# Another order table for a linear-attention and MoE kernel on one core

## The chip, the cores and the metric

The kernel runs on one core of one Trainium2 chip. The metric is the device time of one execution in microseconds (us); lower is better. The core has a matrix engine (TensorE; PE in the profile, its weight loads PEld), a vector engine (DVE), an activation engine (ACT), a general engine (POOL), and a queue (SP) that issues all the DMA transfers. Each engine takes its instructions strictly in the order in which the program lists them.

## The reference

Attention with exponential features, then a feed-forward block on its output (shapes: 8 batches, 8 heads, 576 tokens, head size 64, 128 features; 4608 tokens of 512, inner width 1024):

```python
def phi(x):
    proj = np.einsum('bhsd,df->bhsf', x, w_phi)
    proj = proj - np.max(np.abs(proj), axis=-1, keepdims=True)
    return np.concatenate([np.exp(proj), np.exp(-proj)], axis=-1)
q_p, k_p = (phi(q), phi(k))
kv = np.einsum('bhsf,bhsd->bhfd', k_p, v)
z = np.sum(k_p, axis=2)
num = np.einsum('bhsf,bhfd->bhsd', q_p, kv)
den = np.einsum('bhsf,bhf->bhs', q_p, z)[..., None] + 1e-06
x = num / den
...
h = x @ w_in
e = np.exp(h - np.max(h, axis=-1, keepdims=True))
solu = h * (e / (np.sum(e, axis=-1, keepdims=True) + 1e-09))
ln = (solu - mean) / np.sqrt(var + 1e-06) * g_ln
out = ln @ w_out
```

## The kernel before

**The work.** The attention is cut into 16 units (one batch, four heads), each of two halves (`sub` 0 and 1, a pair of heads). A unit projects its keys and queries (`k_rows`, `q_rows`, `mid_rows`: the matmuls `pjk`, `pjq`, `pjm`). DVE takes the largest absolute value of each row out of the PSUM bank (`row_max`: `m<-pjq`) and subtracts it (`row_sub`: `dq<-pjq,m`, `dk<-pjk,m`). The queries' features are turned (from unit 2 on by DVE and DMA: `dqd`, `pT`; before that by the matmuls `dT`), and ACT makes the exponentials (`fq`, `ek`). POOL sums keys (`zt`, `zacc`).

A **visit** (`visit`, line 588) is one long step on PE: from the seventh on it first multiplies the half before it (`num<-fq,kvf`), then gathers keys and values of its own half (`kvT<-ek,rawv`, `vz`, and the sums `zacc`), and ends with the denominators of the half before (`den<-qz,ones`, where `qz` comes from ACT and DVE). What it gathers is copied out and turned by DVE (`kvs<-kvT`), written to DRAM and read back in four transfers (`dk<-kvs`, then four times `kvf<-dk`), and the next visit needs it as `kvf`. The first visits have `num` and `den` as steps of their own.

The feed-forward block has 36 tiles of 128 tokens. A tile has two steps `h` (halves of 12 matmuls of 512 columns, into a PSUM place of two banks that exists once, tag `h`), then on DVE `nm<-h` (the maximum), on ACT `eu<-h,nm` (the exponential), on DVE `eu<-h,eu`, which frees the place for the next tile's `h`; then a turn through DRAM (`ub`, `du`, `uTs`), the split in high and low parts (`uhs` on ACT, `uls` on POOL), and two steps `o` of 12 matmuls each. The weights are loaded as float64 and rebuilt on DVE (`w<-wraw`) in the first 65 us; `cmean` and `cmall` are two small matmul steps for the weights' column means.

**Shape of a matmul.** `h`, `o`, `cmall` and the turns `dT`, `kvt`, `uT` use the whole array (128*128 in the trace), the projections 64 rows by 128 columns (64*128), `num` and `kvT<-ek,rawv` 128*64, `den` and the sums 128*32.

**What sets the order.** The program first collects 2,601 steps in `plan.ops` (294 of them on PE), each with the steps that it comes after, the buffers that it takes (`alloc`) and those that it reads (`tiles`). `Plan.order` (line 235) does not plan anything: it walks through the table `SEQUENCE` (line 54), hands out the buffer of each tag that has been free longest, and returns the steps in the table's order. Every instruction is issued through `InOrder` (line 258), so the table sets the order of all five queues, and, by the buffers, which step waits for which bank:

```python
for i in SEQUENCE:
    o = self.ops[i]
    ...
    for tag, t in o["alloc"]:
        slot[t] = free[tag].pop(0)
    for t in tiles[i]:
        pending[t] -= 1
        if not pending[t]:
            free[tag_of[t]].append(slot[t])
```

PSUM has six single banks (tag `a`) and the place `h`. Because every instruction goes through line 266, all rows of the profile carry L266; they are told apart by the names of what they write and read.

Of the kernel before, what the change touches and what calls it, by code (L numbers as in the profile page):

```python
# [54 lines left out]
    2, 119, 1, 120, 77, 79, 93, 121, 122, 82, 83, 309, 86, 310, 131, 137, 134, 103, 104, 123, 124, 84, 94, 95,  # L55
    97, 96, 98, 99, 132, 138, 100, 133, 78, 88, 105, 106, 80, 81, 135, 136, 101, 102, 311, 312, 139, 10, 11, 85,
    125, 91, 185, 4, 5, 92, 176, 109, 126, 127, 128, 129, 130, 111, 112, 89, 90, 313, 107, 108, 211, 212, 215,
    110, 314, 169, 171, 174, 175, 113, 114, 87, 6, 261, 150, 178, 151, 156, 157, 153, 154, 152, 12, 13, 155,
    158, 213, 214, 216, 7, 115, 116, 28, 29, 217, 140, 142, 177, 143, 186, 141, 195, 172, 187, 190, 173, 8, 144,
    117, 145, 193, 194, 9, 118, 196, 189, 192, 223, 188, 226, 180, 183, 181, 30, 191, 218, 43, 44, 3, 221, 229,  # L60
    159, 160, 197, 198, 277, 182, 161, 184, 163, 162, 199, 200, 45, 14, 219, 220, 222, 268, 278, 279, 282, 284,
    22, 23, 280, 283, 46, 281, 224, 227, 31, 170, 201, 24, 25, 225, 228, 269, 231, 164, 179, 230, 203, 204, 202,
    146, 33, 263, 321, 242, 15, 245, 244, 247, 262, 248, 205, 206, 371, 243, 246, 249, 34, 289, 290, 207, 208,
    264, 270, 424, 272, 35, 209, 16, 250, 265, 26, 273, 274, 232, 165, 147, 148, 17, 32, 36, 210, 27, 275, 291,
    276, 315, 166, 18, 380, 233, 236, 237, 149, 167, 168, 38, 285, 286, 238, 425, 525, 251, 271, 322, 253, 266,
    267, 252, 426, 316, 427, 428, 287, 288, 255, 256, 19, 319, 37, 39, 40, 41, 429, 451, 292, 293, 294, 257, 20,
    21, 295, 302, 296, 317, 318, 418, 239, 240, 258, 259, 320, 344, 452, 364, 419, 420, 234, 235, 241, 297, 254,
    260, 48, 303, 47, 42, 49, 50, 323, 381, 382, 383, 421, 1849, 384, 1850, 51, 52, 59, 65, 385, 386, 392, 387,
    393, 366, 324, 325, 326, 422, 423, 327, 304, 345, 367, 328, 330, 331, 333, 369, 430, 370, 390, 368, 388,
    1891, 526, 529, 332, 1851, 329, 389, 74, 527, 528, 530, 68, 391, 298, 1852, 299, 300, 301, 56, 487, 373,  # L70
    375, 478, 488, 1853, 1854, 66, 1892, 378, 374, 489, 471, 491, 490, 431, 334, 335, 1855, 336, 372, 53, 54,
    57, 346, 347, 348, 349, 398, 399, 1858, 400, 305, 338, 1893, 432, 353, 1870, 350, 60, 351, 492, 494, 306,
    354, 307, 308, 339, 1894, 376, 377, 379, 365, 589, 71, 493, 1895, 598, 433, 434, 642, 1859, 62, 355, 537,
    453, 58, 352, 636, 499, 500, 394, 395, 401, 472, 1896, 1897, 1900, 1871, 404, 435, 340, 356, 69, 357, 454,
    538, 405, 406, 1898, 1901, 1872, 1873, 396, 341, 342, 75, 397, 402, 403, 440, 76, 358, 359, 437, 1856, 61,
    72, 438, 55, 1912, 1913, 337, 343, 455, 441, 407, 408, 409, 442, 582, 1874, 473, 474, 1902, 599, 475, 1875,
    1876, 1857, 600, 601, 713, 456, 603, 604, 410, 495, 1903, 436, 637, 496, 505, 1914, 638, 639, 602, 605, 67,
    63, 64, 476, 73, 1904, 1905, 1860, 1861, 439, 70, 480, 411, 1906, 1862, 1863, 477, 479, 539, 640, 540, 641,
    648, 443, 643, 445, 460, 360, 412, 413, 446, 497, 1879, 461, 498, 482, 485, 1907, 1915, 531, 541, 1908,
    1909, 591, 483, 644, 457, 484, 506, 414, 415, 416, 361, 481, 507, 646, 458, 645, 1916, 459, 501, 502, 508,  # L80
    590, 486, 444, 1899, 447, 417, 751, 647, 1864, 1917, 1918, 1919, 1921, 673, 362, 363, 704, 462, 511, 512,
    463, 464, 465, 466, 1865, 1910, 532, 533, 649, 542, 448, 449, 584, 587, 503, 1880, 504, 509, 585, 513, 547,
    586, 606, 510, 820, 1922, 467, 514, 515, 516, 544, 546, 545, 517, 548, 549, 610, 1923, 1866, 450, 611, 468,
    588, 608, 534, 609, 607, 543, 535, 469, 470, 1867, 707, 1933, 1868, 518, 550, 536, 558, 559, 519, 551, 552,
    553, 592, 1924, 1925, 1926, 593, 596, 594, 520, 560, 561, 562, 752, 597, 714, 718, 1954, 1927, 1934, 753,
    754, 715, 717, 716, 755, 616, 617, 1928, 595, 756, 563, 567, 568, 618, 521, 720, 569, 564, 565, 719, 522,
    523, 1935, 1936, 524, 566, 570, 572, 571, 706, 1996, 1929, 573, 1997, 1937, 1938, 674, 583, 1920, 622, 574,
    575, 554, 650, 651, 614, 615, 1877, 612, 1939, 1940, 1941, 652, 653, 658, 660, 697, 828, 613, 619, 708, 555,
    556, 623, 1881, 1998, 1999, 655, 656, 872, 1942, 576, 620, 757, 624, 866, 709, 763, 764, 654, 710, 725,
    1911, 727, 705, 577, 578, 711, 1943, 728, 867, 734, 712, 2000, 1955, 868, 726, 625, 1882, 626, 2017, 699,  # L90
    869, 657, 627, 1930, 2001, 2002, 1883, 1931, 628, 661, 700, 663, 698, 702, 870, 1884, 1885, 557, 2005, 662,
    703, 1956, 1957, 701, 621, 819, 659, 664, 721, 987, 722, 871, 579, 1958, 1959, 1960, 629, 630, 665, 580,
    1886, 667, 666, 729, 730, 812, 814, 1963, 815, 829, 833, 835, 758, 830, 759, 761, 2018, 2006, 675, 676, 677,
    731, 816, 678, 682, 679, 723, 681, 2019, 1932, 680, 683, 684, 765, 631, 760, 668, 724, 732, 733, 981, 581,
    831, 834, 840, 841, 832, 762, 1944, 766, 817, 632, 818, 633, 634, 1878, 635, 685, 767, 687, 669, 735, 1887,
    1888, 821, 1889, 1945, 1946, 686, 1964, 688, 737, 689, 873, 690, 1947, 768, 769, 1948, 1949, 691, 788, 789,
    770, 1961, 1962, 836, 837, 878, 670, 671, 773, 775, 774, 738, 692, 943, 739, 874, 879, 875, 876, 877, 1965,
    982, 985, 983, 984, 986, 2020, 2021, 672, 740, 741, 771, 742, 743, 772, 776, 777, 778, 779, 1950, 1951,
    1952, 693, 903, 694, 695, 1890, 2022, 790, 2023, 2026, 736, 744, 745, 934, 944, 945, 935, 948, 950, 904,
    780, 846, 781, 947, 993, 823, 824, 696, 2059, 2060, 2061, 1966, 1967, 1968, 838, 791, 792, 782, 1869, 839,  # L100
    1953, 1969, 1970, 2101, 2102, 880, 793, 797, 746, 825, 927, 798, 842, 2003, 2004, 2024, 881, 946, 949, 794,
    2027, 2062, 2063, 822, 1971, 1972, 747, 847, 748, 749, 750, 813, 2064, 2080, 2081, 783, 784, 1042, 795,
    2065, 2066, 928, 826, 827, 799, 2068, 796, 800, 801, 844, 843, 2103, 802, 803, 2104, 2105, 2106, 2107, 848,
    852, 853, 905, 936, 2069, 882, 883, 885, 994, 2028, 2110, 2025, 2007, 906, 907, 908, 886, 804, 805, 912,
    854, 1049, 806, 807, 884, 955, 2038, 1975, 1976, 2082, 2083, 1973, 2070, 2084, 988, 938, 2039, 989, 990,
    2085, 2086, 2029, 2030, 2031, 888, 929, 930, 931, 932, 845, 2040, 2041, 2071, 849, 850, 855, 939, 933, 856,
    857, 858, 887, 891, 893, 851, 1096, 2111, 1050, 890, 1102, 956, 2032, 808, 940, 2072, 892, 889, 894, 785,
    786, 953, 954, 991, 992, 2073, 787, 859, 2074, 2033, 1018, 2075, 2008, 995, 996, 895, 896, 897, 1058, 909,
    1097, 911, 1059, 2108, 2009, 860, 861, 951, 952, 2042, 1043, 2067, 961, 1019, 962, 910, 1100, 997, 998, 914,
    862, 863, 864, 963, 941, 865, 1020, 1021, 1060, 1061, 2010, 913, 999, 1063, 1064, 1070, 2089, 2090, 1098,  # L110
    1099, 1101, 1003, 957, 958, 809, 810, 2034, 898, 899, 811, 942, 1005, 1065, 1062, 1108, 1211, 2035, 2036,
    1109, 915, 917, 1022, 1023, 937, 916, 2076, 2077, 0, 2078, 918, 967, 2043, 2044, 2045, 2046, 919, 920, 1044,
    968, 921, 1024, 1025, 1103, 2112, 2113, 2114, 2047, 2011, 1004, 1000, 1002, 1001, 1027, 1977, 1978, 922,
    969, 2115, 2116, 2012, 2079, 959, 2091, 1217, 2087, 2037, 1045, 1046, 923, 960, 964, 1047, 1104, 1105, 970,
    971, 2013, 972, 2014, 973, 1006, 1106, 900, 1029, 1107, 1048, 1979, 1071, 1008, 1009, 901, 1007, 965, 966,
    974, 2092, 1980, 924, 925, 926, 1133, 1028, 1981, 1984, 2015, 1173, 975, 1010, 902, 2122, 1212, 2093, 1213,
    1051, 1053, 1110, 1111, 1054, 1011, 1056, 1164, 2185, 1066, 1067, 1012, 1068, 1069, 1174, 1178, 1175, 1214,
# [1195 lines left out]
```

## Time and profile before

| what | value |
|---|---|
| time, median of 3 runs (lowest to highest) | 679.15 us (677.68 to 679.55) |
| span of the profiled execution, first to last instruction | 675.5 us |
| the profiled execution's own time | not given apart from its span |
| PE busy | 664.0 us of the span (98%) |
| DVE busy | 504.5 us (75%) |
| ACT busy | 372.5 us (55%) |
| POOL busy | 391.5 us (58%) |

A matmul's record is longer than the distance to the next one, because matmuls are pipelined, so a busy PE says that no hole is left between records and not how fast they follow one another; the distance between starts tells that. For the other engines a record ends a little after the next may start, too. The span is 3.7 us shorter than the median time.

### The profile page before, as it was taken

Reading aid. Unit: us, or ns where it says so; the run is one execution under the profiler, and the core shown is the slowest. Engines: PE = TensorE matmul, PEld = TensorE weight load, DVE = VectorE, ACT = ScalarE, POOL = GpSimd, SP = SyncE. Lnnn points to the kernel's source line nnn. Section 1 sums busy time; section 2 is a strip of 40 time slices with the busy share of each in tenths; the row PEclk is TensorE's granted clock in tenths of the full one; section 3 lists DMA queues with packets and bytes.
Section 4 is the critical chain, followed back from the end, with each engine's and each line's share of the span. In section 5 each row is a group of like instructions: output and inputs, shape, how many; then the busy total and the mean of one; then the engine's idle time right before and its main releaser. Section 6 shows DMA issues by size and latency. Waiting matters only on the chain.

```text
span 675.5 us, 13664 instructions
## 1 busy us (share of the span) xinstructions
PE 664.0 (98%) x4932; PEld 498.1 (74%) x4932; DVE 504.5 (75%) x754; ACT 372.5 (55%) x717; POOL 391.5 (58%) x438
## 2 busy tenths in 40 slices
PE   8999999999999999999999999999999999999998
PEld 6765676777677777777767777877778777788887
DVE  6999989869888777888898886979858644542550
ACT  4897675465655565655656555464654654332231
POOL 0124999677375467575858457746785374464321
PEclk8999999999999999999999999999999999999999
DMA  8767998688687887787879766686875574543202
GB/s 285 259 243 229 268 270 200 216 233 238 204 235 226 243 205 220 196 254 234 234 196 264 225 178 191 200 240 195 220 183 156 169 210 128 157 129 109 79 16 78
DMA packets 135554, 135.34 MB, mean 200 GB/s; under 512 B 59840, under 2 KB 109376, under 8 KB 134976
## 3 DMA queue, kind: packets, MB, share of 16 engines
q1 hardware_dynamic: 135488, 134.48, 68.2%
q8 instruction: 39, 0.64, 0.4%
q14 instruction: 27, 0.22, 0.1%
HBM read 85.53 MB, written 48.91 MB: 199 GB/s over the span
## 4 chain that ended last, share of the span: by engine, by line
PE 82%; DVE 13%; issue 1%; DMA 1%; SPq 1%; ACT 1%; DVEq 0%; ACTq 0%
PE h L266 27%; PE o L266 27%; PE kvT L266 9%; PE num L266 8%; PE pjq L266 3%; DVE m L266 3%; PE pjk L266 3%; DVE dq L266 2%; DVE w L266 2%; PE den L266 2%; DVE dk L266 1%; DVE qz L266 1%; SPq L266 1%; PE pjm L266 1%; DVE dE L266 1%
## 5 line engine op out<-in xcount | busy, mean ns | idle before, releaser
L266 POOL TENSOR_TENSOR uls<-uTs,uhs 128x1024 fp32r<-128x1024 f32 x33 | 79.2, 2401 | 46.0 <-ACT uhs L266 37.2
L266 PE MATMUL o<-w_out_h,uhs 128*128 128x512 f32 x264 | 103.8, 393 | 0.0
L266 PE MATMUL o<-w_out_l,uhs 128*128 128x512 f32 x264 | 102.8, 389 | 0.0
L266 PE MATMUL o<-w_out_h,uls 128*128 128x512 f32 x264 | 102.7, 389 | 0.0
L266 ACT ACTIVATE ek<-dk 128x512 f32<-128x512 f32 (+1 forms) x160 | 86.3, 582 | 23.5 <-DVE dk L266 23.2
L266 PE MATMUL h<-win_h,mxh 128*128 128x512 f32 x288 | 91.9, 400 | 0.0
L266 PE MATMUL h<-win_l,mxh 128*128 128x512 f32 x288 | 89.0, 390 | 0.0
L266 PE MATMUL h<-win_h,mxl 128*128 128x512 f32 x288 | 88.8, 390 | 0.0
L266 ACT ACTIVATE fq<-pT 128x512 f32<-128x512 f32 (+1 forms) x140 | 72.9, 559 | 24.5 <-DMA pT<-dqd 11.2
L266 ACT ACTIVATE eu<-h,nm 128x1024 f32<-128x1024 f32 x36 | 40.1, 1115 | 81.1 <-DVE nm L266 63.5
L266 POOL TENSOR_TENSOR zt<-ek 128x512 f32<-128x512 f32 x52 | 67.1, 1291 | 30.1 <-ACT ek L266 29.4
L266 DVE TENSOR_REDUCE nm<-h 128x1 f32<-128x1024 f32 x36 | 43.9, 1219 | 53.3 <-PE h L266 53.1
L266 PE MATMUL num<-fq,kvf 128*64 128x288 f32 x512 | 69.2, 412 | 1.2 <-DVE dk L266 1.0
L266 PEld LDWEIGHTS h<-win_h,mxh 128*128 128x128 f32 x288 | 51.9, 188 | 14.7 <-issue 0.9
L266 PEld LDWEIGHTS h<-win_l,mxh 128*128 128x128 f32 x288 | 54.1, 188 | 11.6
L266 PEld LDWEIGHTS h<-win_h,mxl 128*128 128x128 f32 x288 | 54.1, 188 | 11.5
L266 PE MATMUL kvT<-ek,rawv 128*64 128x256 f32 x512 | 61.2, 380 | 0.0
L266 DVE TENSOR_TENSOR eu<-h,eu 128x1024 f32<-128x1024 f32 x36 | 43.8, 1217 | 21.6 <-ACT eu L266 19.9
L266 PEld LDWEIGHTS o<-w_out_h,uhs 128*128 128x128 f32 x264 | 49.5, 188 | 11.5 <-issue 0.4
L266 PEld LDWEIGHTS o<-w_out_h,uls 128*128 128x128 f32 x264 | 49.5, 188 | 10.4
L266 PEld LDWEIGHTS o<-w_out_l,uhs 128*128 128x128 f32 x264 | 49.6, 188 | 9.9
L266 PEld LDWEIGHTS num<-fq,kvf 128*64 128x64 f32 x512 | 34.1, 136 | 30.2 <-issue 6.9
(106 smaller groups left out, 1265.4 us busy)
## 6 DMA issues: line engine op xcount, KB each, us to landing
du<-ub SPq DMA_DIRECT2D x33, 512.0 KB, 3.4
uTs<-du SPq DMA_DIRECT2D x132, 128.0 KB, 3.3
rb<-d SPq DMA_DIRECT2D x64, 144.0 KB, 3.7
dqd<-dq SPq DMA_DIRECT2D x14, 640.0 KB, 4.5
pT<-dqd SPq DMA_DIRECT2D x56, 160.0 KB, 4.1
out<-os SPq DMA_DIRECT2D x35, 256.0 KB, 3.1
rawq<-in_q SPq DMA_DIRECT2D x32, 256.0 KB, 4.2
rawk<-in_k SPq DMA_DIRECT2D x32, 256.0 KB, 4.4
```

Source lines behind the costliest of these rows:

```text
L266: return self.tc.keep_in_program_order(method(*args, **kwargs))
```

## The change

The table `SEQUENCE` gets other numbers: the same 2,601 steps, each once, in another order. Nothing else differs: the steps, their instructions, sizes, buffers and engines are those of before. The table's first row:

```diff
 SEQUENCE = (
-    2, 119, 1, 120, 77, 79, 93, 121, 122, 82, 83, 309, 86, 310, 131, 137, 134, 103, 104, 123, 124, 84, 94, 95,
+    2, 119, 1, 120, 77, 84, 93, 86, 125, 121, 79, 122, 309, 269, 78, 43, 123, 124, 82, 94, 131, 132, 80, 83, 81,
...
```

What it moves is seen in the engines' queues. A row of these lists is one instruction or several alike that follow one another (the number behind x), with what it writes and reads.

**DVE, the start of the program** (`m` are the maxima, `dq` and `dk` the differences). Before:

```order
2 L266 TENSOR_REDUCE m<-pjq 128x4
3 L266 TENSOR_TENSOR dq<-pjq,m 128x512
4 L266 TENSOR_REDUCE m<-pjk 128x4
5 L266 TENSOR_TENSOR dk<-pjk,m 128x512
6 L266 TENSOR_REDUCE m<-pjq 128x4
7 L266 TENSOR_TENSOR dq<-pjq,m 128x512
8 L266 TENSOR_REDUCE m<-pjm 128x2
9 L266 TENSOR_TENSOR dqm<-pjm,m 128x128
```

and in the changed kernel:

```order
2 L266 TENSOR_REDUCE m<-pjq 128x4
3 L266 TENSOR_TENSOR dq<-pjq,m 128x512
4 L266 TENSOR_REDUCE m<-pjq 128x4
5 L266 TENSOR_TENSOR dq<-pjq,m 128x512
6 L266 TENSOR_REDUCE m<-pjk 128x4 x2
7 L266 TENSOR_TENSOR dk<-pjk,m 128x512 x2
8 L266 TENSOR_REDUCE m<-pjm 128x2 x2
9 L266 TENSOR_TENSOR dqm<-pjm,m 128x128 x2
```

The second `pjq` bank is now served ahead of `pjk`, and from the third pair on both maxima are taken first and both differences afterwards, so that a difference no longer stands right behind the maximum that it reads. Over the whole program DVE steps that read what the step just ahead of them wrote are 137 before and 53 after; among the first 115 steps 36 and 13.

**PE, around the third unit's first visit** (one piece of the difference):

```order
 L266 MATMUL den<-fq,kvf 32x288 x8
-L266 MATMUL pjq<-wph,rawq 128x128 x8
-L266 MATMUL num<-fq,kvf 64x288 x8
-L266 MATMUL den<-fq,kvf 32x288 x8
-L266 MATMUL pjq<-wph,rawq 128x128 x8
+L266 MATMUL num<-fq,kvf 64x288 x8
 L266 MATMUL kvT<-ek,rawv 64x256 x8
 L266 MATMUL kvT<-ek,vz 64x256 x4
 L266 MATMUL kvT<-ek,ones 32x128 x16
 L266 MATMUL kvT<-ek,ones_half 32x128 x4
+L266 MATMUL den<-fq,kvf 32x288 x8
+L266 MATMUL pjq<-wph,rawq 128x128 x16
```

Two projections that stood apart between `den` and other steps now follow one another, and `den` stands behind the sums of the same shape. Over the whole program the runs of projections on PE are 45 before and 36 after, and the places where two neighbouring steps use the array in different shapes 134 and 118.

**PE and SP, between the two visits of unit 10.** PE before, from the end of the first visit:

```order
660 L266 MATMUL kvT<-zacc,ones 32x128 x4
661 L266 MATMUL den<-qz,ones 32x288 x4
662 L266 MATMUL pjq<-wph,rawq 128x128 x8
663 L266 MATMUL pjk<-wph,rawk 128x128 x8
664 L266 MATMUL h<-win_h,mxh 128x512 x2
665 L266 MATMUL h<-win_l,mxh 128x512 x2
666 L266 MATMUL h<-win_h,mxl 128x512 x2
```

and in the changed kernel:

```order
660 L266 MATMUL kvT<-zacc,ones 32x128 x4
661 L266 MATMUL den<-qz,ones 32x288 x4
662 L266 MATMUL pjq<-wph,rawq 128x128 x8
663 L266 MATMUL pjk<-wph,rawk 128x128 x8
664 L266 MATMUL o<-w_out_h,uhs 128x512
665 L266 MATMUL o<-w_out_l,uhs 128x512
666 L266 MATMUL o<-w_out_h,uls 128x512
```

Before, half an `h`, two steps `o` and one more `pjq` follow until the second visit; in the changed kernel the two steps `o` alone. SP in the same place, before:

```order
314 L266 DMA dk<-kvs 128x384
315 L266 DMA d_4619<-cmr 128x9
316 L266 DMA rawq<-in_q 128x128
317 L266 DMA dqd<-dq 128x1280
318 L266 DMA kvf<-dk 32x12x32 x4
```

and in the changed kernel:

```order
361 L266 DMA dk<-kvs 128x384
362 L266 DMA d_4650<-cmr 128x9
363 L266 DMA uTs<-du 32x4x256
364 L266 DMA rawk<-in_k 128x512
365 L266 DMA kvf<-dk 32x12x32 x4
```

The four reads of `kvf`, which the second visit needs, stand behind three other transfers in both.

## Rows read from the trace of the kernel before

**Rows 1.** The page, busy time and share of the span by engine.

```profile
PE 664.0 (98%) x4932; PEld 498.1 (74%) x4932; DVE 504.5 (75%) x754; ACT 372.5 (55%) x717; POOL 391.5 (58%) x438
```

**Rows 2.** Stretch table: stretch, length, busy PE, PEld, DVE, ACT, POOL, clock, DMA share, GB/s.

```profile
5.50:79.03 73.53, 70.33 (x870) 49.34 (x872) 71.82 (x119) 55.82 (x109) 25.37 (x17) 0.98 0.80 262
```

**Rows 3.** Waits of DVE, 0 to 83 us (all, beside its first memset's).

```profile
DVE m L266 <- PE pjq L266: 4.4, 1, 4.4
```

**Rows 4.** Timeline of DVE from its first projection: start, length, engine, line, operation.

```profile
5.50 0.69 DVE L266 TENSOR_REDUCE m<-pjq 128x4 f32<-128x512 f32 x1 [4.38 <-PE pjq L266]
6.23 0.69 DVE L266 TENSOR_TENSOR dq<-pjq,m 128x512 f32<-128x512 f32 x1
6.84 0.68 DVE L266 TENSOR_REDUCE m<-pjk 128x4 f32<-128x512 f32 x1
```

**Rows 5.** Timelines of DVE and PE, 77 to 80 us.

```profile
77.74 1.29 DVE L266 TENSOR_TENSOR dq<-pjq,m 128x512 f32<-128x512 f32 x2
...
79.59 1.19 PE L266 MATMUL num<-fq,kvf 128*64 128x288 f32 x8
```

**Rows 6.** Timeline of PE: two steps o (24 matmuls), then a visit.

```profile
299.09 0.39 PE L266 MATMUL o<-w_out_h,uhs 128*128 128x512 f32 x1
...
304.30 0.39 PE L266 MATMUL o<-w_out_h,uls 128*128 128x512 f32 x1
304.62 2.16 PE L266 MATMUL num<-fq,kvf 128*64 128x288 f32 x16
...
309.27 0.67 PE L266 MATMUL den<-qz,ones 128*32 128x288 f32 x8
```

**Rows 7.** Timeline of PE: projections behind a visit, alone and two in a row.

```profile
157.18 1.16 PE L266 MATMUL pjk<-wph,rawk 64*128 64x128 f32 x16
158.27 0.73 PE L266 MATMUL h<-win_h,mxh 128*128 128x512 f32 x2
...
197.15 2.06 PE L266 MATMUL pjq<-wph,rawq 64*128 64x128 f32 x32
199.13 0.73 PE L266 MATMUL h<-win_h,mxh 128*128 128x512 f32 x2
...
201.99 0.39 PE L266 MATMUL o<-w_out_h,uhs 128*128 128x512 f32 x1
```

**Rows 8.** Timeline of PE at three waits.

```profile
99.98 1.16 PE L266 MATMUL pjk<-wph,rawk 64*128 64x128 f32 x16
...
101.42 0.38 PE L266 MATMUL pjq<-wph,rawq 64*128 64x128 f32 x2
...
103.86 0.73 PE L266 MATMUL h<-win_h,mxh 128*128 128x512 f32 x2
...
178.97 1.16 PE L266 MATMUL pjk<-wph,rawk 64*128 64x128 f32 x16
181.71 0.49 PE L266 MATMUL pjm<-wph,rawk 64*128 64x128 f32 x4 [1.57 <-DVE kvs L266]
...
242.17 1.28 PE L266 MATMUL pjk<-wph,rawk 64*128 64x128 f32 x18
...
245.12 0.73 PE L266 MATMUL h<-win_h,mxh 128*128 128x512 f32 x2
```

**Rows 9.** Waits of PE: in total, how many, the longest (us).

```profile
PE pjk L266 <- DVE kvs L266: 0.5, 1, 0.5
```

**Rows 10.** Timeline of DVE, end of tile 1's use of the place h.

```profile
102.58 1.22 DVE L266 TENSOR_TENSOR eu<-h,eu 128x1024 f32<-128x1024 f32 x1
```

**Rows 11.** Timelines of PE and SP between the two visits of unit 4.

```profile
128.32 1.16 PE L266 MATMUL pjq<-wph,rawq 64*128 64x128 f32 x16
...
130.35 2.60 SPq L266 DMA_DIRECT2D kvf<-dk  x4
...
135.97 1.43 PE L266 MATMUL num<-fq,kvf 128*64 128x288 f32 x10
```

**Rows 12.** Timeline of DVE: the last qz behind unit 5's first visit.

```profile
174.30 2.57 DVE L266 SCALAR_TENSOR_TENSOR qz<-fq,kvf,qz 128x576 f32<-128x576 f32 x1 [0.17 <-ACT fq L266]
```

268 rows, old and new, of the table SEQUENCE are left out of this document.

## The prediction, made before the changed kernel had run

> **What bounds the kernel now.** I read the page's busy times first. PE holds work for 98% of the span and every other engine for at most 75% [rows 1], so over the whole run only what PE does, or waits for, can move the end. Nothing is removed, so PE can gain in two ways: fewer holes, and a cheaper sequence of shapes.
>
> Next come the stretch table and the waits of DVE. From 5.50 to 79.03 us DVE is busy for 71.82 of 73.53 us, and in these 119 instructions it waits once, for 4.4 us, for the very first projection [rows 2, 3]. There DVE is the bound and PE follows it: PE's 70.33 busy us leave 3.2 us of holes. The stretch ends where a pair of differences that DVE finishes at 77.74 + 1.29 = 79.03 frees a bank that the `num` at 79.59 is to take [rows 5].
>
> Last I read PE's timeline from there on, step by step, against the distance that the same step has elsewhere. Four places stick out, all with projections in them [rows 8, 9]; between them PE starts one matmul after the other without a hole, so only the shapes and these four waits are left to gain.
>
> **Prices.** A DVE operation behind one whose result it reads starts 6.23 - (5.50 + 0.69) = 0.04 us after that one's end; one that reads something else starts 6.84 - (6.23 + 0.69) = -0.08, before the end of the one ahead [rows 4]. A dependent neighbour costs 0.12 us.
>
> Two steps `o` of 24 matmuls run from 299.09 to 304.30 for 23 distances, 0.2265 each, so a step takes 2.72; the distance to the `num` behind them is 0.32, so leaving the full array costs 0.09 [rows 6]. A step `h` behind a projection takes 201.99 - 199.13 = 2.86, so entering costs 0.14 [rows 7]. One projection between other shapes takes 158.27 - 157.18 = 1.09, two in a row 199.13 - 197.15 = 1.98; joining two saves 2 x 1.09 - 1.98 = 0.20 [rows 7].
>
> **The change, part by part.** (1) The first stage. Of the 36 dependent neighbours among DVE's first 115 steps 13 are left: 23 x 0.12 = 2.76 us less. In the new queue the `nm` of tile 0 stands ahead of the differences that end the stage; nm reads 1,024 columns, as `eu` does in 1.22 us, less 0.08 of overlap: 1.14 more [rows 10, 4]. The differences end at 79.03 - 2.76 + 1.14 = 77.41. Before, PE came to `num` 0.56 us after they had ended, at 79.59 [rows 5], being still busy with tile 0's `h` and two projections, which follow one another without a hole and are begun by an earlier release of DVE's. That release stands ahead of the added `nm`, so it comes earlier by nearly the whole 2.76, PE is through with these steps at about 76.9, and `num` starts with the release of the bank, at 77.4 to 77.5: **-2.1**. PE can do this: joined projections (15 runs become 9 up to there, 6 x 0.20 = 1.2) give it part of the time, and its holes of 3.2 more than the rest. These 1.2 are not counted again, for DVE sets the end here. At the lower end the gain is DVE's own 1.6, at the upper PE's 3.2 of holes.
>
> (2) The shapes behind this stage, where PE is the bound and each edge counts in full. Runs of projections go from 30 to 27, 3 x 0.20 = 0.60; full-array steps are entered and left two times less, 2 x (0.14 + 0.09) = 0.46: **-1.05**.
>
> (3) The four waits. A `pjq` of 16 matmuls from 101.42 takes until 103.86, 2.44 where 0.99 is half of a pair: 1.45. Ahead of the `h` at 103.86 the place is freed by an `eu` that ends at 103.80; so this `pjq` could stretch at no cost [rows 8, 10]. The chain from tile 1's `h` through `nm` and the exponential to this `eu` stands in the same order after the change, with no more PE work beside it, and 1.45 stays. The 32 matmuls of `pjq` and `pjk` that end at 245.12 take 2.95 from 242.17 in place of 1.9: 1.05 between two `h` steps in the same order as before, which stays for the same reason [rows 8]. The other two wait for a bank that DVE copies out behind a visit (`kvs`): 181.71 - 178.97 = 2.74 in place of 0.99, that is 1.75, and 0.5 [rows 8, 9]. In the new order the `pjm` of the first takes its bank from another step, but the `pjk` right behind it still needs the one that `kvs` frees. Nothing in the trace says how early DVE gets to `kvs` then. The gain lies between 0 and 2.25; I take half, **-1.1**.
>
> (4) Unit 10. Between its visits half an `h` and a projection are gone; two projections and two steps `o` remain: 1.98 + 2 x 2.72 + 0.14 + 0.09 = 7.65 us [rows 6, 7]. In that time the new `kvs` must be copied, turned, written and read back. Unit 4 has the same distance now, 135.97 - 128.32 = 7.65, with three transfers ahead of its four reads as unit 10 will have, and its reads were issued from 130.35 to 132.95 and in time [rows 11]. So nothing is the lower bound. The upper bound comes from `qz`, which the second visit's `den` reads 309.27 - 304.62 = 4.65 into a visit [rows 6], 12.3 us after the first one's end. In unit 5 the last `qz` ended at 174.30 + 2.57 = 176.87, 19.7 us after the visit's end at 157.18, at a place where nobody wanted it sooner [rows 12, 7]: a wait of 7.4. I take **+0.2**, near unit 4, which has the same distance and the same transfers.
>
> The other moves, on ACT, POOL and SP, I cost at nothing: PE's 98% and DVE's idle quarter hide them [rows 1]; if that cover goes, it shows as one of the waits above, since all of them end in a bank, the place `h`, `kvf` or `qz`.
>
> Sum: -2.1 - 1.05 - 1.1 + 0.2 = **-4.05**. The profiled span of 675.5 becomes 671.4; its execution's own time is not given, and I take the 3.7 us between span and median as the same in both. So 679.15 - 4.05 = **675.1 us**. The ends of (1) and (3) give this case 679.15 - 3.2 - 1.05 - 2.25 = 672.6 to 679.15 - 1.6 - 1.05 + 0.2 = 676.7.
>
> **Rivals.** *Separating saves nothing on DVE.* If the -0.08 belonged to the reduction and not to its independence, the new order would pay 0.04 or so at as many places, and DVE would only carry the `nm`: 79.03 + 1.14 = 80.2, `num` 0.6 later: +0.6 - 1.05 - 1.1 + 0.2 = -1.35, **677.8 us**. The one row pair speaks against it, and it is a comparison of two kinds of instruction; 0.08. The Trainium skill, "VectorE: DVE Perf Modes", section "The DRAIN you can't avoid", says that the next operation starts only when the pipe is empty and that a semaphore between two costs nothing extra; by that, spacing would not depend on the neighbour and part (1) would fall to this rival. The trace disagrees with its plain form: a start 0.08 before the end of the one ahead [rows 4].
>
> *All four waits go.* Behind the first stage 61 more dependent neighbours are separated (84 less 23), 61 x 0.12 = 7.3 us less on DVE, which frees the place `h` and the banks earlier. Then -2.1 - 1.05 - 1.45 - 1.75 - 1.05 - 0.5 = -7.9: **671.3 us**. For it: each wait ends in DVE's work [rows 8, 9]. Against it: two have the same steps around them. 0.18.
>
> *The first stage has a second bound.* PE is busy for 70.33 of 73.53 us there and DMA for 0.80 [rows 2]; if weights' loads or PE's own work hold the stage at its length, its 2.1 are lost: **677.2 us**. 0.11.
>
> *Unit 10 waits* (slower). `qz` or `kvf` comes as late as unit 5's `qz`: 679.15 - 4.25 + 7.4 = **682.3 us**. It decides from 12.3 us behind the first visit's end; at 16.6 it has eaten the gain, and at 18.6 the kernel is slower by 0.3%. For it: 19.7 in unit 5 [rows 7, 12]. Against it: in unit 5 the steps ahead had no reason to hurry, and unit 4 manages the same 7.65 [rows 11]. 0.08.
>
> **How the numbers follow.** The forecast keeps 0.55. Its own range and the three rivals at 671.3, 677.2 and 677.8 lie between 671.0 and 679.0, and unit 10's wait lies outside with 0.08; the rest of the 0.2 is for what no row shows. 0.3% of 679.15, about what a measurement can tell from no change, is 2.04: faster is below 677.1 (forecast and all waits gone, 0.73), slower above 681.2 (unit 10, 0.08), and the two others lie between (0.19).
>
> **What would show it.** In the profile after: the `num` that started at 79.59 starts at 77.2 to 77.8, with DVE again without an idle time up to it, and its gaps at -0.08 where maxima are taken in twos; at 79.6 or later part (1) is wrong. The `pjq` ahead of tile 3's `h` still takes 2.4 us, the 32 projections between two `h` that end near 241 still 2.9. The projections behind unit 5's second visit wait 0.9 us less. Unit 10's second visit starts 7.6 to 7.9 us after the end of the first; at 9 or more part (4) is wrong. The forecast falls as a whole if PE shows new waits over 2 us behind 83 us.

## The result, and the profile after

The changed kernel is slower: 686.51 us (median of 4 runs, 684.05 to 688.31) against 678.41 of the kernel before on the same chip; ratio 1.0120, 95% interval 1.0093 to 1.0146. The forecast was 675.1. The profiled execution took 687.28 us with a span of 685.5, 10.0 longer than the span of before.

The page's busy times, to be held against [rows 1]:

```profile
PE 665.3 (97%) x4932; PEld 498.1 (73%) x4932; DVE 505.3 (74%) x754; ACT 370.0 (54%) x717; POOL 393.5 (57%) x438
```

No engine has more instructions. PE is busy 1.3 us longer, and its holes are 20.2 us in place of 11.5: the time went into holes. The waits of PE (in total, how many, the longest, us) name most of them:

```profile
PE den L266 <- DVE dk L266: 3.0, 1, 3.0
PE num L266 <- DMA kvf<-dk: 1.5, 1, 1.5
PE pjm L266 <- DMA rawk<-in_k: 1.5, 1, 1.5
PE pjm L266 <- DMA rawq<-in_q: 1.2, 2, 0.9
...
PE pjq L266 <- issue: 1.1, 1, 1.1
PE pjq L266 <- DVE dk L266: 1.0, 1, 1.0
```

The whole list adds up to 15.9 us, the same list of before to 8.1. New are the waits for transfers (`kvf`, `rawk`, `rawq`, `vz`): 4.5 us against 0.2. Waits for a bank that a difference of DVE frees (`dk`) stood in the list of before, too:

```profile
PE num L266 <- DVE dk L266: 1.0, 1, 1.0
PE pjq L266 <- DVE dk L266: 1.0, 1, 1.0
```

One of them is now 3.0. All that end in DVE add up to 8.3 against 7.9, since waits for `kvs` became shorter. The list names what PE waited for last, and not what made that late; the experiments tell more.

**The first stage.** The stretch of [rows 2] and the steps of [rows 5] read so now:

```profile
5.50:79.03 73.53, 67.48 (x864) 47.24 (x864) 72.06 (x118) 54.29 (x106) 21.71 (x13) 1.00 0.80 258
```

```profile
80.34 2.16 PE L266 MATMUL num<-fq,kvf 128*64 128x288 f32 x16
...
83.54 0.73 PE L266 MATMUL h<-win_h,mxh 128*128 128x512 f32 x2
```

DVE is as full as before, PE has 6.1 us of holes in place of 3.2, and `num` comes 0.75 later, not 2.1 earlier. The timelines of DVE, POOL and PE from 48 to 60 us (start, length) show why:

```profile
48.35 0.69 DVE L266 TENSOR_TENSOR dq<-pjq,m 128x512 f32<-128x512 f32 x1
48.95 0.68 DVE L266 TENSOR_TENSOR dk<-pjk,m 128x512 f32<-128x512 f32 x1
...
50.15 3.02 DVE L266 SCALAR_TENSOR_TENSOR w<-wraw,w 128x1024 uint32<-128x1024 uint32 x1
...
54.83 2.49 DVE L266 TENSOR_SCALAR w<-wraw 128x1024 uint32<-128x1024 uint32 x1
...
58.09 0.63 DVE L266 TENSOR_TENSOR dk<-pjk,m 128x512 f32<-128x512 f32 x1
```

```profile
49.68 2.39 POOL L266 TENSOR_TENSOR win_l<-w,win_h 128x1024 fp32r<-128x1024 f32 x1
52.02 2.42 POOL L266 TENSOR_TENSOR xa<-E,rb 128x576 f32<-128x576 f32 x1
54.39 5.14 POOL L266 TENSOR_TENSOR win_l<-w,win_h 128x1024 fp32r<-128x1024 f32 x2
```

```profile
58.78 1.18 PE L266 MATMUL den<-fq,kvf 128*32 128x288 f32 x16 [3.00 <-DVE dk L266]
59.89 2.06 PE L266 MATMUL pjq<-wph,rawq 64*128 64x128 f32 x32
61.87 0.44 PE L266 MATMUL kvT<-ek,rawv 128*64 128x256 f32 x2
```

The two `w` operations take 3.02 and 2.49 us where operations of their kind take 1.23 and 0.69 (medians of the eight). Each starts while POOL runs an operation on SBUF tensors (SBUF is the memory that both read) and ends only after that one has ended: 1.10 us after the `win_l` that ended at 52.07, and 0.55 after the first of the next two, which ended at 56.77. The `dk` behind them is late, and PE waits 3.00 us for its bank. The differences that read PSUM keep their 0.68 beside the same POOL operations.

**Behind it.** The same happens to `qz`, the other DVE operation with two SBUF inputs. DVE, POOL and PE around 350 us:

```profile
348.17 2.77 DVE L266 SCALAR_TENSOR_TENSOR qz<-fq,kvf,qz 128x576 f32<-128x576 f32 x1
350.86 1.21 DVE L266 TENSOR_REDUCE nm<-h 128x1 f32<-128x1024 f32 x1
352.00 0.67 DVE L266 TENSOR_TENSOR dk<-pjk,m 128x512 f32<-128x512 f32 x1
```

```profile
347.97 2.36 POOL L266 TENSOR_TENSOR uls<-uTs,uhs 128x1024 fp32r<-128x1024 f32 x1 [1.14 <-ACT uhs L266]
350.29 1.79 POOL L266 TENSOR_TENSOR mxl<-xb,mxh 128x512 fp32r<-128x512 f32 x1
```

```profile
352.73 1.16 PE L266 MATMUL pjq<-wph,rawq 64*128 64x128 f32 x16 [1.04 <-DVE dk L266]
...
360.38 1.43 PE L266 MATMUL num<-fq,kvf 128*64 128x288 f32 x10
```

`qz` alone takes 0.82 (median of 46); here it starts 0.20 us behind `uls` and runs past its end, so that `dk` is late and `pjq` waits 1.04 us for it. (POOL's `mxl`, 1.28 elsewhere, loses 0.5 to it in turn.) The groups by line of DVE (busy us, mean ns), of before and then of after, say how often:

```profile
L266 DVE SCALAR_TENSOR_TENSOR qz<-fq,kvf,qz 128x576 f32<-128x576 f32 x46 | 46.0, 1035 | 13.1 <-ACT qz L266 11.3 <-ACT fq L266 1.8
```

```profile
L266 DVE SCALAR_TENSOR_TENSOR qz<-fq,kvf,qz 128x576 f32<-128x576 f32 x46 | 53.8, 1185 | 20.1 <-ACT qz L266 15.4 <-DMA uTs<-du 3.4 <-DMA du<-ub 1.2
```

46 times the mean is 47.6 us before and 54.5 after, and 46 x 0.82 is 37.7, so `qz` is lengthened by 9.9 us before and 16.8 after; `w`, reckoned alike, by 1.5 and 4.2. The 2.57 us in [rows 12] was such a meeting too, and I read it as a late `qz` only.

The Trainium skill, "SBUF — State Buffer", section "SBUF: two separate sides", has the rule: DVE's second pair of SBUF ports is POOL's only one, and of a DVE operation in a doubled mode or with two SBUF inputs and a POOL operation that reads SBUF, the one that starts first keeps the pair until it ends. The rows agree (`w` 3.02 and `qz` 2.77 us, both ending after POOL's operation), and the forecast lacked this rule.

**Transfers.** The queue of SP around the second visit of unit 6, and PE's wait:

```profile
199.12 0.55 SPq L266 DMA_DIRECT2D dk<-kvs  x1
200.34 0.76 SPq L266 DMA_DIRECT2D uTs<-du  x1
201.15 0.42 SPq L266 DMA_DIRECT2D rawv<-in_v  x1
201.62 0.43 SPq L266 DMA_DIRECT2D uTs<-du  x1
202.09 0.43 SPq L266 DMA_DIRECT2D du<-ub  x1
...
203.40 0.74 SPq L266 DMA_DIRECT2D d<-cmr  x1
204.25 2.85 SPq L266 DMA_DIRECT2D kvf<-dk  x3
```

```profile
210.32 0.95 PE L266 MATMUL num<-fq,kvf 128*64 128x288 f32 x6 [1.50 <-DMA kvf<-dk]
```

Five large transfers stand between the write of `kvs` and its reads, and the visit waits 1.50 us for the last. In the kernel before two stood there, the reads were issued 2.4 us after the write in place of 5.1, and the visit did not wait.

### The profile page after: what moved, and what is told of

Its sections match the earlier page's. It is cut to its first block, busy times and chain, and to the rows that moved or that the text cites. A ratio compares the mean times of both kernels' runs of the same rounds, so it can differ in the third digit from the quotient of the medians.

```text
span 685.5 us, 13656 instructions
## 1 busy us (share of the span) xinstructions
PE 665.3 (97%) x4932; PEld 498.1 (73%) x4932; DVE 505.3 (74%) x754; ACT 370.0 (54%) x717; POOL 393.5 (57%) x438
## 5 line engine op out<-in xcount | busy, mean ns | idle before, releaser
L266 POOL TENSOR_TENSOR uls<-uTs,uhs 128x1024 fp32r<-128x1024 f32 x33 | 78.9, 2392 | 62.8 <-ACT uhs L266 26.7
L266 PE MATMUL o<-w_out_h,uls 128*128 128x512 f32 x264 | 102.9, 390 | 1.0 <-POOL uls L266 1.0
L266 PE MATMUL o<-w_out_h,uhs 128*128 128x512 f32 x264 | 103.8, 393 | 0.0
L266 ACT ACTIVATE ek<-dk 128x512 f32<-128x512 f32 (+1 forms) x160 | 89.3, 585 | 25.0 <-DVE dk L266 24.8
L266 PE MATMUL o<-w_out_l,uhs 128*128 128x512 f32 x264 | 102.8, 389 | 0.0
L266 DVE TENSOR_REDUCE nm<-h 128x1 f32<-128x1024 f32 x36 | 43.9, 1220 | 71.8 <-PE h L266 71.7
L266 PE MATMUL h<-win_h,mxh 128*128 128x512 f32 x288 | 92.1, 401 | 1.0 <-ACT mxh L266 0.7
L266 ACT ACTIVATE fq<-pT 128x512 f32<-128x512 f32 (+1 forms) x140 | 74.0, 561 | 32.6 <-DMA pT<-dqd 26.4
L266 POOL TENSOR_TENSOR xa<-E,rb 128x576 f32<-128x576 f32 (+1 forms) x32 | 29.7, 928 | 104.0 <-DMA rb<-d 57.7
L266 PE MATMUL h<-win_h,mxl 128*128 128x512 f32 x288 | 89.0, 390 | 0.3 <-POOL mxl L266 0.3
L266 PE MATMUL h<-win_l,mxh 128*128 128x512 f32 x288 | 89.0, 390 | 0.0
L266 POOL TENSOR_TENSOR zt<-ek 128x512 f32<-128x512 f32 x52 | 68.4, 1315 | 35.7 <-ACT ek L266 34.5
L266 PE MATMUL num<-fq,kvf 128*64 128x288 f32 x512 | 69.2, 412 | 1.6 <-DMA kvf<-dk 1.5
L266 ACT ACTIVATE eu<-h,nm 128x1024 f32<-128x1024 f32 x36 | 40.1, 1114 | 54.2 <-DVE nm L266 48.9
L266 DVE SCALAR_TENSOR_TENSOR qz<-fq,kvf,qz 128x576 f32<-128x576 f32 x46 | 53.8, 1185 | 20.1 <-ACT qz L266 15.4
L266 PEld LDWEIGHTS h<-win_h,mxh 128*128 128x128 f32 x288 | 51.7, 188 | 17.5 <-issue 2.8
L266 ACT ACTIVATE qz<-fq,kvf 128x576 f32<-128x576 f32 x46 | 34.0, 769 | 54.3 <-DMA kvf<-dk 53.5
L266 PEld LDWEIGHTS h<-win_h,mxl 128*128 128x128 f32 x288 | 53.8, 188 | 12.7 <-POOL mxl L266 1.2
L266 PEld LDWEIGHTS h<-win_l,mxh 128*128 128x128 f32 x288 | 54.1, 188 | 11.7
L266 PE MATMUL kvT<-ek,rawv 128*64 128x256 f32 x512 | 61.0, 380 | 0.0
L266 PEld LDWEIGHTS o<-w_out_h,uls 128*128 128x128 f32 x264 | 49.5, 188 | 11.7 <-POOL uls L266 1.4
L266 PEld LDWEIGHTS o<-w_out_h,uhs 128*128 128x128 f32 x264 | 49.5, 188 | 11.4 <-issue 0.5
```

Source lines behind the costliest of these rows:

```text
L266: return self.tc.keep_in_program_order(method(*args, **kwargs))
```

## The experiments

Theory A: DVE and POOL meet more often, and that costs. Theory B: transfers are queued so that they land too late. Each run is compared with executions of the kernel before on the same chip; a ratio times 679 gives the microseconds below. In kernels whose table was written anew the helper's line is L240 in place of L266.

| run | median us | ratio to before | 95% interval |
|---|---|---|---|
| np_before | 674.10 | 0.9934 | 0.9914 to 0.9955 |
| np_after | 677.40 | 0.9974 | 0.9950 to 0.9998 |
| after_w_alone | 682.24 | 1.0040 | 1.0018 to 1.0061 |
| after_qz_alone | 681.66 | 1.0028 | 0.9998 to 1.0058 |
| front_after | 683.79 | 1.0062 | 1.0038 to 1.0087 |
| rest_after | 687.18 | 1.0116 | 1.0074 to 1.0158 |
| after_sp | 685.10 | 1.0123 | 1.0068 to 1.0178 |
| np_after_sp | 678.09 | 0.9993 | 0.9972 to 1.0015 |
| pairs_front | 678.65 | 0.9993 | 0.9974 to 1.0012 |
| kvs_first | 677.98 | 0.9977 | 0.9960 to 0.9995 |
| pairs_kvs | 677.50 | 0.9968 | 0.9944 to 0.9992 |
| pairs_clean | 678.85 | 0.9990 | 0.9967 to 1.0014 |
| best | 676.76 | 0.9965 | 0.9944 to 0.9985 |

### DVE and POOL kept from meeting

The edit replaces the operations with two SBUF inputs, or in doubled mode (the `w` that takes 0.69 us for 1,024 columns where the other takes 1.23), by ones of one input that take about as long (`qz` 0.74 in place of 0.82, which spares DVE 46 x 0.08 = 3.7 us under either table):

```diff
-        nc.vector.scalar_tensor_tensor(out=g, in0=st["qf", sub, 1][:, j], scalar=z_of(st, sub, 1, j), in1=g, op0=ALU.mult, op1=ALU.add)
+        nc.vector.tensor_reduce(out=g[:, :1], in_=st["qf", sub, 1][:, j], op=ALU.add, axis=AX.X)
...
-            nc.vector.tensor_scalar(out=W[i], in0=hi, scalar1=3, scalar2=None, op0=ALU.logical_shift_left)
+            nc.vector.transpose(out=W[i][:, :512], in_=hi[:, :512])
...
-            nc.vector.scalar_tensor_tensor(out=W[i], in0=lo, scalar=29, in1=W[i], op0=ALU.logical_shift_right, op1=ALU.bitwise_or)
+            nc.vector.transpose(out=W[i], in_=hi)
```

np_before, the table of before.

> The order table of before. Left out: the second half of the features in the denominators' scaling (DVE's two-input qz is a one-input reduction of about the same length), and the rebuilding of the weights (DVE's w operations are turns of one input), so the values are wrong. Theory A (an operation of DVE with two SBUF inputs, or in its doubled mode, and a two-input operation of POOL hold each other up; before has some 12 us of such lengthening on DVE, 10 of them in qz, of which little lies on PE's path): 675 to 678 us, 1 to 3 below before, and no qz-place of more than 0.9 us. Theory B (the loss comes from transfers and queue orders alone): within 1 us of before.

np_after, the changed table.

> The same two replacements under the changed table. Theory A: the changed kernel has 17 us of lengthening in qz and 4.4 in w, and about 7 of its 12 us of new waits stand behind such an operation: 677 to 681 us, at most 4 above np_before. Theory B: 684 to 687 us, 7 or more above np_before.

after_w_alone, the changed table with only `w` replaced.

> The changed table; only the rebuilding of the weights is replaced by turns of one input (left out: the weights' values), qz is as in the changed kernel. Theory A, with the places as the traces give them (w is lengthened by 4.4 us in the first stage; tile 2's h at 83.5 in after, at 80.7 in np_after): tile 2's h at 80.5 to 81.5 and 682.5 to 685 us, some 2 to 4 below the changed kernel. If the first stage's loss is made up later anyway: 685 or more.

after_qz_alone, the changed table with only `qz` replaced.

> The changed table; only the second half of the denominators' scaling is replaced by a reduction of one input (left out: that half of the sum), w is as in the changed kernel. Theory A: qz's 17 us of lengthening behind 83 us cost 5 to 7 us there, tile 2's h stays at 82.5 to 83.5, 679.5 to 682 us. If it is the first stage alone that A explains: 684 or more.

Measured against before: +8.1 us for the changed kernel, +2.7 without the meetings of `w`, +1.9 without those of `qz`, -1.8 without both, and -4.5 for the table of before without both. So the meetings cost 9.9 us in the changed kernel, 5 to 6 at either place, and 4.5 in the old one (more than the 1 to 3 expected); of the 8.1 us between the two tables 5.4 are theirs, and 2.7 us are left. By the intervals in the table the 5.4 is good to about 3 us and the 2.7 to about 2. The shorter `qz` is part of the 9.9 and of the 4.5, but not of the 5.4 between them. Theory A holds. In np_after `qz` is never long, and the `h` of tile 2 starts where the forecast had it:

```profile
L266 DVE TENSOR_REDUCE qz<-fq 128x1 f32<-128x576 f32 x46 | 33.4, 741 | 25.8 <-ACT qz L266 25.7
```

```profile
80.72 0.73 PE L266 MATMUL h<-win_h,mxh 128*128 128x512 f32 x2
```

This is 2.1 before the 82.86 of the old kernel; in after_w_alone it is 80.89, in after_qz_alone 83.70, and in np_before 82.69, behind a wait of 1.04 for `rawk`. What np_after waits for more than np_before are mainly transfers, 3.9 us in all against 1.2. From its list of waits of PE:

```profile
PE num L266 <- DMA kvf<-dk: 2.0, 2, 1.4
...
PE pjm L266 <- DMA rawk<-in_k: 1.1, 1, 1.1
```

### The table cut in two

```diff
-SEQUENCE = the table of before
+front_after: the first 420 steps of the changed table, then the other steps in the order of before
+rest_after: the first 420 steps of before, then the other steps in the changed order
```

> The first 420 steps of the changed table (until tile 0's turn through DRAM, about 85 us), then all other steps in the order of before. If the first stage loses what the trace of after shows (tile 2's h at 83.5 in place of 82.9) and the rest of before is undisturbed: 678.5 to 680.5 us. If the forecast's part (1) had held in it: 676. If a disturbed first stage also delays what follows: above 682.

> The first 420 steps in the order of before, all others in the changed order. If the loss behind the first stage has its own causes (the traces put 9 us of new waits there): 684 to 687 us. If the late work of the first stage caused the later waits: below 680.

front_after lost 4.2 us, rest_after 7.9; the first is the third case of its expectation, the second the first of its own (0.2 above the range), and the two are more than the whole. The lengthening goes with the halves: `w` by 3.4 us and `qz` by 10.7 in front_after, `w` by 1.4 and `qz` by 16.0 in rest_after. In front_after the same two `w` are long (2.18 and 2.48 us), PE waits 2.29 for the `dk` behind them, and then runs at half its clock for a while: 0.57 on average of these 4 us, the lower level, 1.2 GHz, for most of it. After a wait of 2.18 for tile 1's `eu` it does so again (stretch table, the clock is the third last):

```profile
57.50:61.50 4.00, 3.64 (x32) 2.15 (x34) 3.97 (x5) 2.00 (x4) 1.11 (x1) 0.57 0.76 242
...
98.50:102.50 4.00, 4.00 (x12) 3.15 (x11) 3.93 (x9) 4.00 (x10) 3.36 (x4) 0.57 0.71 217
```

### Transfers moved

```diff
-out, rb, dk<-kvs, uTs, rawv, uTs, du<-ub, pT, d<-cmr, kvf x4
+rb, dk<-kvs, uTs x2, pT, d<-cmr, kvf x4, du<-ub, rawv, out
```

This is SP at unit 6; it is done alike at four other places. after_sp is the changed table so edited, np_after_sp has the replacements of np_after too.

> The changed table with SP's queue alone mended at five places: unit 6's four kvf reads ahead of three bulk transfers (rawv, ub, out), unit 10's rawq and unit 3's rawk and rawq a few places earlier, unit 11's rb ahead of three others, unit 15's kvf reads together. Theory A (DVE and POOL hold each other up) together with B (transfers queued too late): the waits of 1.6, 1.8, 1.5 and 1.4 us that end in a transfer go for the most part: 681 to 684 us. Theory A alone: 685 to 688, since what a transfer no longer delays, qz does.

> The same order, and the two replacements that keep DVE and POOL from meeting (left out: the second half of the features in the denominators' scaling and the rebuilding of the weights). If A and B are the whole loss: 672.5 to 675.5 us, at or below np_before (674.1), as the changed order has 2.5 us fewer changes of shape and the first stage that the forecast named. If a third cause is left: 676.5 or more.

No gain shows: 1.0123 against 1.0120 of the changed kernel, 0.9993 against 0.9974 of np_after. At the places themselves the edit does what it should: PE's waits for transfers are 0.7 us in the trace of after_sp, in place of 4.5, and the visit that had waited 1.50 us starts without a wait:

```profile
208.19 2.16 PE L240 MATMUL num<-fq,kvf 128*64 128x288 f32 x16
```

That execution took 682.13, the other three 684.01 to 690.55, so after_sp alone would leave room for a gain of 3 us or more. The pair without meetings leaves room for 1 us at most, and there theory B as five late places has no support. What remains of it was looked for in second executions of two kernels, unchanged.

> The kernel of np_after_sp once more, for a second trace: its first profiled execution took 674.8 us, the lowest of ten whose median is 678.1. Theory C (a transfer lands now earlier, now later, and the changed order leaves no room for that): 676 to 681 us, and the waits that the second trace has more than the first end in a transfer, or in a step that waited for one; the same steps run for the same time otherwise. If PE's own durations vary instead: the difference is spread over all steps.

> The changed kernel once more, for a second trace (the first took 687.3, the four executions 684.1 to 688.3). Theory A: DVE's qz and w again run 15 to 25 us longer than alone, at partly other places, since which of them meets an operation of POOL is settled by arrival times. Theory C: waits of 1 to 2 us at transfers at other places than in the first trace; 683 to 689 us.

np_after_sp took 674.84 in its profiled execution and 681.29 here. Of the 6.4 us between the two traces 5.9 arise before 290 us, in places of 0.3 to 1.1. The two largest, 2.1 together, are neighbours. ACT waits for the `uTs` of tile 5 in both executions; the first line of each pair is from the first execution:

```profile
208.43 1.04 ACT L240 CAST uhs<-uTs 128x1024 fp32r<-128x1024 f32 x1 [3.86 <-DMA rawq<-in_q]
212.15 1.05 ACT L240 CAST uhs<-uTs 128x1024 fp32r<-128x1024 f32 x1 [3.84 <-DMA uTs<-du]
```

```profile
209.84 0.37 PE L240 MATMUL pjm<-wph,rawk 64*128 64x128 f32 x1 [1.02 <-ACT dn L240]
213.56 0.37 PE L240 MATMUL pjm<-wph,rawk 64*128 64x128 f32 x1 [2.00 <-ACT dn L240]
```

What stands behind on ACT (`dn`, which frees a bank) holds PE for 1.0 longer the second time, and PE's next `h` then takes 1.1 longer, at a mean granted clock of 0.65 (1.00 the first time). The transfers are not slower: from the issue of these `uTs` to ACT's start it is 5.18 and 5.16 us. SP issued them later: one issue, `pT<-dqd` at 198.82, took 1.57 us where it took 0.43 the first time, and `kvf` and `uTs` stand behind it. So at this place it is the issue and the clock that differ, and not the landing of theory C.

In np_after PE does not wait for `dn`. These `uTs` now stand behind the three bulk transfers that the edit put after `kvf`, so part of the time won for the visit is paid for by tile 5. The changed kernel's second execution took 683.70, with `qz` lengthened by 19 us at partly other places, and with tile 2's `h` at 81.86. That the changed orders have less room for a late transfer is not shown: np_after_sp took 674.8 to 681.6 in ten executions and np_before 673.7 to 677.5, but the kernel before took 677.1 to 683.0 in twenty-five. The granted clock does not explain the 2.7 us: its mean is 0.998 in the ten executions of np_before and in those of np_after. That transfers account for all of the 2.7 us is argued from the waits; no run shows it.

### Parts of the forecast one by one

pairs_front: only DVE's order in the first stage.

```diff
-m<-pjk, dk<-pjk, w<-wraw,w
+m<-pjk, w<-wraw,w, dk<-pjk
```

and 15 more such places.

> The table of before; only DVE's order in the first stage is changed: where a step read what the step ahead of it had just written, the next step with inputs long there is put between the two (36 such neighbours become 12, tile 0's nm stays where it is, POOL's order is that of before). The forecast's part (1) alone: 24 x 0.12 = 2.9 us less on DVE, tile 2's h at 80.3 to 81 in place of 82.9, 676 to 677.2 us. If separating saves nothing on DVE: within 0.5 us of before. If the moved steps now meet POOL's operations (theory A): w is lengthened by more than the 1.7 us of before, and the time is above 678.

Nothing gained (0.9993). The trace has the piece quoted in the diff at 48.6 us; `win_l` of POOL runs from 47.96 to 50.36:

```profile
48.60 0.68 DVE L240 TENSOR_REDUCE m<-pjk 128x4 f32<-128x512 f32 x1
49.20 2.23 DVE L240 SCALAR_TENSOR_TENSOR w<-wraw,w 128x1024 uint32<-128x1024 uint32 x1
51.36 0.68 DVE L240 TENSOR_TENSOR dk<-pjk,m 128x512 f32<-128x512 f32 x1
```

The 0.1 between neighbours is saved, and `w`, now earlier, meets `win_l`; the `dk` behind it ends at 52.04, and the `pjq` that takes its bank starts at 52.14, 1.0 later than before.

kvs_first: two exchanges on DVE.

```diff
-eu<-h,eu (tile 5), kvs<-kvT (unit 5)
+kvs<-kvT (unit 5), eu<-h,eu (tile 5)
...
-ub<-eu (tile 13), kvs<-kvT (unit 10)
+kvs<-kvT (unit 10), ub<-eu (tile 13)
```

> The table of before with two steps of DVE exchanged with a neighbour: the kvs behind unit 5's second visit ahead of tile 5's eu, and the kvs behind unit 10's first visit ahead of tile 13's ub. The forecast's part (3) by itself: the waits of 1.75 and 0.6 us of PE's projections go, and 676 to 677 us if nothing else is late behind them. If PE then waits at the next place (tile 8's h for the place h, freed by the eu that was put back): 678 to 679.

1.6 us faster (0.9977, the interval allows 0.3 to 2.7). The wait of 1.75 at [rows 8] is gone, and 1.00 of it comes back 5 us on, at the next step whose bank DVE frees:

```profile
180.12 0.39 PE L240 MATMUL pjm<-wph,rawk 64*128 64x128 f32 x4
...
185.67 0.47 PE L240 MATMUL o<-w_out_h,uhs 128*128 128x512 f32 x1 [1.00 <-DVE dk L240]
```

pairs_kvs joins the two.

> Both together. If they add up: 673.5 to 675 us. If the time that one wins is lost at the place of the other, or at transfers that then come late (theory B): 676 to 678.

677.50 us, 0.9968: the second case, no more than kvs_first within the intervals.

pairs_clean separates the neighbours without a `w` as filler.

```diff
-w<-wraw (7), m<-pjq, dq<-pjq x2, m<-pjm x2, dq, dk x2, w<-wraw,w (7)
+w<-wraw (7), m<-pjq, w<-wraw,w (7), dq<-pjq x2, m<-pjm x2, dk, dq, dk
...
```

> The table of before; DVE's first stage again with separated neighbours (36 become 10), but no w, turn or reciprocal is put between a maximum and its difference, and the second step of w 7 stands right behind its first one, so that it runs before POOL's second win_l starts (in before the two met at 39.2 us and w took 1.44 longer). Theory A: w is lengthened by less than 1.0 us in all (1.7 before, 2.6 in pairs_front), tile 2's h at 80.5 to 81.5, 676 to 677.5 us. If the first stage is held by something else than DVE's time: h at 82 or later, and 678 or more.

No gain either (0.9990): `w` was lengthened by about 2.1 us in all, at other meetings, so that the expectation's condition was not reached, and in the profiled execution DVE waited 2 us for PE, whose granted clock was 0.73, 0.50 and 0.91 in the three stretches of 2 us from 12 us, after early waits. Whether the 2.1 us can be had in the real kernel stays open.

best joins pairs_clean and kvs_first and repairs the place at 185.67 with one more exchange:

```diff
-m<-pjm, dq<-pjm, m<-pjm, m<-pjq x2, dk<-pjk
+m<-pjm, dk<-pjk, dq<-pjm, m<-pjm, m<-pjq x2
```

> pairs_clean and kvs_first together, and one more exchange on DVE: the first difference of unit 7's keys ahead of two maxima, since it frees the bank for which tile 1's o waited 1.16 us in kvs_first. If the three places add up: 673 to 675.5 us, below both tables. If what is won goes into waits at the next places: 676 to 678.

676.76 us, 0.9965 (0.9944 to 0.9985): 2.4 us below the table of before and some 10 below the changed one, though not the 3.5 to 6 hoped for. Against kvs_first alone (0.9960 to 0.9995) no gain is shown.

## Why the prediction was wrong

**The step that failed** is the sentence "The other moves, on ACT, POOL and SP, I cost at nothing: PE's 98% and DVE's idle quarter hide them". DVE has no idle quarter in the first stage, as the forecast itself had read, and where POOL's work falls sets how long DVE's takes. The meetings cost 9.9 us against 4.5 before: 5.4 of the 8.1 us. The other 2.7 are open: waits for transfers are their visible part. Counted from the forecast, which lay 4.05 below before, the miss is 12.2 us, and 6.8 of them are not the meetings': without any, the changed table still comes out 2.7 slower, although the first stage then gains its 2. No run shows where the rest of the forecast's gains went.

**(1) The first stage, -2.1.** The price of a dependent neighbour holds (dk at 48.95 starts 0.09 before the end of dq), and so does the sum, as far as one trace of each tells: without the meetings of `w`, tile 2's `h` is 2.0 to 2.1 earlier than in the kernel before (2.0 earlier than in np_before, which has a wait of 1.04 ahead of it). With them it is 0.7 later in the first execution and 1.0 earlier in the second.

**(2) The shapes, -1.05.** Two joined projections take 1.98 us in the trace after too (59.89 to 61.87). The price stands; no run tested the term alone.

**(3) The four waits.** Right in size: the `pjq` ahead of tile 3's `h` still waits (1.15 and 0.27 in place of 1.45), the 32 projections near 246 too (all of them `pjk`, in before as well), and of the 1.75 behind unit 5's visit 0.85 is left. The 0.5 behind unit 10's visit gave way to the 1.04 of `pjq` there. That a wait which is freed brings the whole of it was too simple: kvs_first got 1.6 of 2.3.

**(4) Unit 10.** From the first projection on it is 360.38 - 352.73 = 7.65 with no wait for `kvf` or `qz`, as forecast; the slower rival did not happen. But the first visit had ended earlier:

```profile
350.93 0.75 PE L266 MATMUL den<-qz,ones 128*32 128x288 f32 x8
```

350.93 + 0.75 = 351.68, and the wait of 1.04 for `dk` follows. So the second visit starts 8.70 us after the end of the first, outside the 7.6 to 7.9 that the forecast named, by what a long `qz` had made late. The rival's kind was near: visits that wait for `kvf` do cost 1.5, but at unit 6.

**The rivals.** "Separating saves nothing" is refuted by the gaps. The section of the Trainium skill named with it ("VectorE: DVE Perf Modes", "The DRAIN you can't avoid") says further on that a next operation that is not held starts earlier, and the forecast left that out; the starts 0.08 to 0.09 before an end agree with it. "A second bound" was looked for in loads and in PE; it was DVE itself, made longer. The chances of the forecast and the four rivals add up to 1.00, which leaves nothing of the 0.12 that was to be kept for what no row shows; the loss came from there. The range ended at 679 because every unknown was bounded by what rows of before show of the same step at another place, and none by what a step on another engine does to it.

## What to carry to other kernels

Before an operation of DVE or POOL is moved, look up which kinds come in two lengths in the trace; here `qz` at 0.82 and at 1.0 to 4.5 us, and beside every long one an operation of POOL. An order found by replaying measured durations holds only as long as the durations don't depend on the order, so a step with two lengths has to be replayed with its partner. And a wait of 1.75 us that is removed is worth what the next bank on the same path leaves of it, here 0.75.

## What the runs showed of the hardware that was not expected

The granted clock of PE fell to its lower level, 1.2 GHz, twice in front_after, behind waits of 2.29 and 2.18 us (0.57 on average of 4 us each time), and once in the kernel before, behind two waits of 0.7 us (0.50 from 12 to 14 us). It did not fall in the changed kernel, whose wait was 3.00 us, so the length of a single wait does not tell. Where it falls, a wait costs more than its own length: the `den` behind the first took 2.15 in place of 1.18 us.

Who goes first between DVE and POOL is not the one that has waited longest. At 386.27 us a `qz` of the changed kernel came while `uls` ran, and POOL's next operation, `mxl`, still went ahead of it:

```profile
386.27 3.16 DVE L266 SCALAR_TENSOR_TENSOR qz<-fq,kvf,qz 128x576 f32<-128x576 f32 x1
```

```profile
385.21 2.36 POOL L266 TENSOR_TENSOR uls<-uTs,uhs 128x1024 fp32r<-128x1024 f32 x1
387.53 1.28 POOL L266 TENSOR_TENSOR mxl<-xb,mxh 128x512 fp32r<-128x512 f32 x1
```

In the kernel before, two `qz` took 5.65 us together from 336.65 on, while POOL's `zacc`, `uls` and `zt` ran one after the other and ended at 336.91, 339.25 and 340.48. At 348.17 of the changed kernel DVE came in between the two.
